# Attention, mixture of experts and feed-forward on one core: another expert order, another order of attention's small products, other queues for the first pairs

## Chip, core and metric

The kernel runs on one core of one Trainium2 chip. The time is the device time of one execution in microseconds (us). Each execution has its own time; the profile comes from one further execution. TensorE is called PE, VectorE DVE, ScalarE ACT, GpSimd POOL, and SyncE SP; a name with a q behind it (SPq, ACTq) is the queue or sequencer of that engine.

## What is computed

Three layers in a row on 2304 tokens of 512 values (4 batches of 576 tokens, 8 heads of 64). Cut to its core:

```python
q_rot, k_rot = rotate(q), rotate(k)                       # rotary positions
attn = softmax(q_rot @ k_rot.T / sqrt(64));  x = attn @ v # per batch and head
x = x.transpose(0, 2, 1, 3).reshape(2304, 512)

xn, en = x / (norm(x) + 1e-6), expert_emb / (norm(expert_emb) + 1e-6)
logits = xn @ en.T / tau;  expert_idx = argmax(logits, 1)  # 8 experts
for e in range(8):                                         # each token goes to one expert
    out[expert_idx == e] = gate * (relu(x @ w1[e]) @ w2[e])  # 512 -> 1024 -> 512

h = out @ w_in;  g = where(h > 0, h, exp(min(h, 0)) - 1);  y = g @ w_out  # 512 -> 2048 -> 512
```

The reference, evaluated on the inputs that are used, sends 6, 709, 173, 0, 3, 691, 722 and 0 tokens to experts 0 to 7. After the first three of the four batches the counts are 6, 706, 173, 0, 3, 118, 722 and 0.

## The kernel before

**Order.** All work is put down as small tasks, `add(time, function, arguments)`, with a due time in abstract units. `emit` sorts them by that time and writes them out, so the numbers set the order of the instructions on every engine and on every queue. An engine takes its instructions in this order. `OFF` is a table of corrections to due times, and of choices such as which engine does a step.

**Attention** runs in 16 pairs of heads, 9 units apart. For pair p: `load` brings q and k (and both with their halves swapped) on SP's queue; `rope` is six steps on POOL or DVE; `hi` (ACT) and `lo` (DVE) split the result into two float16 parts; `stack` copies these with six DMAs into one of four operand buffers. `sc` (line 327) makes score products, and `sc_max` (line 337, DVE) takes the largest of each row; nine of these per pair. `m_turn` (lines 347 and 348, "the turn of the maxima") transposes the maxima on PE, ACT copies them (line 350), and two small DMAs (lines 352 and 353, on ACT's queue) put them beside the operands. Then come nine `st` (lines 363 and 364), the scores again in transposed form with the maximum subtracted, each followed by an exponential on ACT (line 365). `pv` makes, for each of five blocks of keys, the product with v (line 401) and right behind it the sums of the exponentials (line 409). `o_out` copies the result, `o_turn` (line 427, "the turn of the output") transposes it on PE, and `epi` (lines 442 to 451, DVE) divides by the sums. sc, st and both turns take their place in PSUM from a ring of three double banks (`pair`): each use waits until the use three places back in the ring has been read.

**Routing** follows each batch: logits, the place of each token in its expert's list (`r_*`), and a scatter of the tokens. `tab_early` (after three batches) and `tab_head`, `tab_visits`, `tab_compact` (after four) work out on DVE which expert each visit serves. A **visit** is one block of up to 128 tokens of one expert. The first five visits are settled by `tab_early`. `tab_head` ranks the experts by their blocks that are left (`rk`, 0 for the most; the expert that the early visits ended with gets rank 0), and subtracts 3.5 from ranks of 4 and over, so that small experts stand between large ones. With the counts above there are 22 visits, and their experts are 1 six times, 0, 5 six times, 4, 6 six times, 2 twice. There is room for 25; those from the 19th on are skipped on PE by a branch if they aren't used, and small products (line 1083) stand in.

**Expert stage.** Visit j has `mm1` (lines 1057 to 1059, 96 products), `relu` on ACT and DVE, `mm2` (lines 1094 to 1096, 24 products) and `y_out`. On PE, mm2 of a visit follows mm1 of the next one. Where a visit's expert is another than that of the visit before, `w_load` brings its 4 MB in eight pieces (lines 1009 and 1012, SP's queue) into staging buffers, and `w_conv` splits each into float16 parts on ACT (line 1029) and DVE (line 1031). There are eleven staging buffers at first. One after the other they are given up for the third layer's weights (list `until`), at the due time of the first weight chunk that is put there. From unit 36.3 of this stage (two units are one visit) there are two.

**The third layer's weights** come as 64-bit floats in 32 chunks. `widen` turns a chunk into float16 parts, in five steps that go ACT (line 960), DVE (lines 962 to 965), ACT (968), POOL or DVE (971 to 974, chunks 16 and up), ACT (981), POOL (983). `WT` gives each chunk its due time, in units of the stage. Chunks 16 to 29 stand at 23.6, 30, 30.9, and so on up to 42.2. Two chunks can be under way.

**Third layer.** Nine groups of 256 tokens: `ff1` (lines 1139 to 1141), `elu`, `ff2` (1191 to 1193), `fold`, `store`.

## Time and profile before

| | us |
|---|---|
| median of 3 runs | 1009.29 |
| lowest and highest | 1006.53, 1009.57 |
| the profiled execution: its time | 1010.61 |
| the profiled execution: its span, first to last instruction | 1008.8 |
| PE busy in it | 901.2 |
| DVE, ACT, POOL busy | 669.7, 502.3, 546.3 |

The span falls into these stages: the first pairs' way to PE, up to about 44 us; attention until about 356; the change to the experts, which overlaps it, until 372.5; the visits until about 634; and the third layer. All times in rows are us from the span's start. A row of a timeline gives start, duration, engine, line, operation, what is written and read, how many instructions are merged in the row and, in brackets, how long the engine had stood idle before and what ended that. MH are the maxima, ms their transposed copy; most other things lie in one large tile, arena. PEclk in a table of stretches is the granted clock of PE as a share of full speed (1.0 is 2.4 GHz, 0.5 is 1.2 GHz).

### The profile page before, as it was taken

How to read it: one execution, taken by the hardware profiler on the slowest of the kernel's cores; microseconds unless marked ns; L12 is line 12 of the kernel's file. 1: busy time of each engine (PE TensorE's matmuls, PEld its weight loads, DVE VectorE, ACT ScalarE, POOL GpSimd, SP SyncE). 2: the span in 40 equal slices, each digit the busy share in tenths (PEclk: the TensorE clock that was granted, in tenths of full speed). 3: DMA queues.
4: the chain of work that ended last, by engine and by line, in shares of the span. 5: the costliest groups of instructions: out<-in, count | busy, mean ns of one | idle time of the engine just before them, and what ended most of it. 6: DMA issues, size and time to landing. Idle time of an engine off the chain costs nothing. (4 is left out here: it accounts for less than half of the span.)

```text
span 1008.8 us, 24500 instructions
## 1 busy us (share of the span) xinstructions
PE 901.2 (89%) x9398; PEld 655.4 (65%) x9398; DVE 669.7 (66%) x1070; ACT 502.3 (50%) x858; POOL 546.3 (54%) x652
## 2 busy tenths in 40 slices
PE   3398999998989779999999876998999999999994
PEld 0154555554445467776776652887888888888884
DVE  8556757867868547778786874775665565664651
ACT  1244464464464633565665444645555555555540
POOL 6475565685643203424428544366776765766640
PEclk8588999999999979999999987999999999999998
DMA  7554465584463844997997674401201202201000
GB/s 261 152 166 107 129 156 136 142 200 127 133 144 104 251 85 144 328 249 200 260 304 175 192 203 92 123 2 43 64 22 43 64 22 43 65 22 44 22 22 21
DMA packets 127094, 127.65 MB, mean 127 GB/s; under 512 B 71272, under 2 KB 105064, under 8 KB 126960
## 3 DMA queue, kind: packets, MB, share of 16 engines
q1 hardware_dynamic: 118000, 97.68, 37.5%
q0 software_dynamic: 8352, 27.62, 8.5%
q8 instruction: 76, 1.25, 0.5%
q10 hardware_dynamic: 608, 0.63, 0.2%
q14 instruction: 58, 0.48, 0.2%
HBM read 79.15 MB, written 17.35 MB: 96 GB/s over the span
## 5 line engine op out<-in xcount | busy, mean ns | idle before, releaser
L1139 PE MATMUL banks<-arena 128*128 128x256 f16 x576 | 157.1, 273 | 2.4 <-ACT arena L1154 2.4
L1141 PE MATMUL banks<-arena 128*128 128x256 f16 x576 | 157.1, 273 | 0.0
L1140 PE MATMUL banks<-arena 128*128 128x256 f16 x576 | 157.1, 273 | 0.0
L365 ACT ACTIVATE arena<-banks 128x576 f32<-128x576 f32 x144 | 89.8, 652 | 125.8 <-PE banks L364 108.5
L1191 PE MATMUL banks<-arena 128*128 128x256 f16 x504 | 138.2, 274 | 5.5 <-DVE arena L1206 5.5
L1174 DVE TENSOR_TENSOR arena<-arena 128x896 f16<-128x896 f32 x72 | 79.9, 1110 | 89.0 <-ACT arena L1170 84.0
L1192 PE MATMUL banks<-arena 128*128 128x256 f16 x504 | 138.2, 274 | 0.0
L1193 PE MATMUL banks<-arena 128*128 128x256 f16 x504 | 138.2, 274 | 0.0
L1170 ACT ACTIVATE arena<-arena 128x896 f16<-128x896 f32 x71 | 67.5, 951 | 122.7 <-POOL arena L1167 121.4
L337 DVE TENSOR_REDUCE MH<-banks 128x1 f16<-128x576 f32 x144 | 103.2, 751 | 34.1 <-PE banks L327 32.3
L1059 PE MATMUL banks<-arena 128*128 128x128 f16 x704 | 122.4, 222 | 1.5 <-DVE arena L1031 1.5
L1057 PE MATMUL banks<-arena 128*128 128x128 f16 x704 | 122.5, 222 | 0.0
L1058 PE MATMUL banks<-arena 128*128 128x128 f16 x704 | 122.5, 222 | 0.0
L1164 POOL TENSOR_TENSOR arena<-arena 128x256 f32<-128x256 f32 x67 | 54.1, 808 | 91.4 <-DVE arena L1161 91.4
L983 POOL TENSOR_TENSOR arena<-arena 128x896 f16<-128x896 f32 (+1 forms) x32 | 51.6, 1611 | 86.1 <-ACT arena L981 65.7
L401 PE MATMUL banks<-arena 128*64 128x256 f32 (+9 forms) x768 | 90.9, 362 | 4.6 <-DVE arena L377 4.6
L363 PE MATMUL banks<-arena 128*128 128x288 f16 (+1 forms) x320 | 79.5, 299 | 3.5 <-DVE l L523 2.2
L327 PE MATMUL banks<-arena 64*128 64x288 f16 (+1 forms) x320 | 48.5, 313 | 37.0 <-DVE MH L337 16.2
L1095 PE MATMUL banks<-arena 128*128 128x512 f16 x176 | 70.2, 399 | 10.2 <-DVEq L993 9.6
L364 PE MATMUL banks<-arena 128*128 128x288 f16 (+1 forms) x320 | 78.5, 294 | 0.0
L1094 PE MATMUL banks<-arena 128*128 128x512 f16 x176 | 69.8, 396 | 6.0 <-ACT arena L1069 4.4
L377 POOL TENSOR_TENSOR arena<-arena 128x576 f16<-128x576 f32 x26 | 30.2, 1162 | 79.8 <-ACT arena L365 79.8
(238 smaller groups left out, 2285.2 us busy)
## 6 DMA issues: line engine op xcount, KB each, us to landing
arena<-in_w_dram SPq DMA_DIRECT2D x48, 512.0 KB
arena<-in_qk_dram SPq DMA_DIRECT2D x30, 576.0 KB
arena<-in_wo_dram SPq DMA_DIRECT2D x32, 256.0 KB
arena<-in_wi_dram SPq DMA_DIRECT2D x16, 512.0 KB
arena<-arena SPq DMA_DIRECT2D x32, 216.0 KB
yreg<-arena POOLq DMA_DIRECT2D x25, 260.0 KB, 4.0
arena<-arena SPq DMA_DIRECT2D x32, 144.0 KB
arena<-in_vp_dram SPq DMA_DIRECT2D x16, 256.0 KB
```

The costliest lines, as they stand in the source:

```text
L337: nc.vector.tensor_reduce(out=MH1[p % 2][:, c:c + 1], in_=t[:, :, 0:288], op=ALU.max, axis=AX.XY, negate=True)
L365: nc.scalar.activation(P32[:, (9 * p + i) % RP].rearrange("p (c n) -> p c n", c=2), t[:, :, 0:288], AF.Exp, scale=2.0)
L401: nc.tensor.matmul(o[64 * e:64 * e + 64, c, 0:QC[c].stop - QC[c].start], lhsT=w, rhs=x[:, QC[c]], start=first and n == 0, stop=end and n = ...
L1057: nc.tensor.matmul(o[:, fc], lhsT=w[:, 0, a], rhs=x[:, k], start=k == 0, stop=False)
L1058: nc.tensor.matmul(o[:, fc], lhsT=w[:, 0, a], rhs=x[:, 4 + k], start=False, stop=False)
L1059: nc.tensor.matmul(o[:, fc], lhsT=w[:, 1, a], rhs=x[:, k], start=False, stop=k == 3)
L1139: nc.tensor.matmul(o[:, v], lhsT=wih[k][:, f0:f0 + 128], rhs=z[:, :, k], start=k == 0, stop=False)
L1140: nc.tensor.matmul(o[:, v], lhsT=wih[k][:, f0:f0 + 128], rhs=z[:, :, 4 + k], start=False, stop=False)
L1141: nc.tensor.matmul(o[:, v], lhsT=wil[k][:, f0:f0 + 128], rhs=z[:, :, k], start=False, stop=k == 3)
L1191: nc.tensor.matmul(y, lhsT=a, rhs=b, start=u + f + n == 0, stop=False)
L1192: nc.tensor.matmul(y, lhsT=a, rhs=w[:, 1, WB[i - 1]], start=False, stop=False)
L1193: nc.tensor.matmul(y, lhsT=q[:, 1, f, GB[i - 1]], rhs=b, start=False, stop=u + f == 4 and n == len(m) - 1)
```

## The change

**Expert order.** `tab_head` gets two more steps on DVE: the expert of rank 2 has 7 added to its rank and so is visited last. With the counts above the visits become 1 six times, 0, 5 six times, 4, 2 twice, 6 six times. Chunks of the third layer get other due times: 26 and 27 at 23.2 and 29, then 16 to 25, 28 and 29 from 34 to 43.35, 0.85 apart. The staging buffers whose place they take are so kept longer: seven are there until 33.9, and three or more until 40.7.

**Attention.** The sums become a task `ps` of their own, due up to 0.8 later than the product with v, so that one st mostly stands between them. The turn of the maxima moves from 2.9 to 3.68 units after the last maximum, and the turn of the output from 14.7 to 15.05, so that both stand right in front of the next sc. From the second pair on, the two DMAs of the maxima are issued by SP and not by ACT.

**First pairs.** The order of what all queues do for pairs 0 to 3 is another: c_prep's conversion of constants goes to ACT, the rest of c_prep and the norm of the expert embeddings move behind; all six rope steps of pair 0, and three of pair 2, are DVE's; pair 1 has a buffer of its own for its float16 parts; pair 0's stack is eight DMAs, four on SP and four on ACT; three warm-up products fewer. The score products of pair 1 stand behind the first st of pair 0 and not before it.

```diff
+    def c_copy():
+        nc.scalar.copy(c16, cft[:, 0:512])
     def c_prep():
-        nc.vector.tensor_copy(c16, cft[:, 0:512])
...
         if w == 0:
-            hlt[p] = at("hl", F16, 4, 576)
+            hlt[p] = at("P", F16, 4, 576, add=32256) if p == 1 else at("hl", F16, 4, 576)
...
     def stack(p):
+        if p == 0:
+            for e, eng in ((0, nc.sync), (1, nc.scalar)):
+                a, o = slice(64 * e, 64 * e + 64), slice(64 - 64 * e, 128 - 64 * e)
+                eng.dma_start(out=t[a, e, 0:3:2, 0:576], in_=h[a, 0:3:2])
...
-        nc.scalar.dma_start(out=d[64:65, 0, 1], in_=ms[0:5])
-        nc.scalar.dma_start(out=d[0:1, 1, 1], in_=ms[5:10])
+        eng = nc.sync if p else nc.scalar
+        eng.dma_start(out=d[64:65, 0, 1], in_=ms[0:5])
+        eng.dma_start(out=d[0:1, 1, 1], in_=ms[5:10])
...
+        po[p, kt] = ones
+    def ps(p, kt):
+        o, ones, end = obank, po.pop((p, kt)), kt == PVO[-1]
         for c in range(2):
...
+        pl_ = tbv(864, 8)
+        nc.vector.tensor_scalar(pl_, rk, 2.0, 7.0, op0=ALU.is_equal, op1=ALU.mult)
         nc.vector.tensor_tensor(rk, rk, ps_, op=ALU.add)
+        nc.vector.tensor_tensor(rk, rk, pl_, op=ALU.add)
...
-    add(-25.5, warm, OFF.get('WN', 13))
+    add(-25.5, warm, 10)
...
-        u, w = (z - 13.45, 1) if p else (z - 19, .3)
+        u, w = {0: (-19, .3), 1: (.6, .6), 2: (6.2, .95)}.get(p, (z - 13.45, 1))
...
-        add(u + w * (UT[4] + (2.9 if p else 1.3)), m_turn, p)
+        add(u + w * (UT[4] + (3.68 if p else 1.3)), m_turn, p)
...
+            add(z + t + (.01 if p == NP - 1 else ST5[kt]), ps, p, kt)
-        add(z + (11.8 if p < NP - 1 else 10.6), o_out, p)
-        e = z + (14.7 if p < NP - 1 else 11.4)
+        add(z + (12.3 if p < NP - 1 else 10.6), o_out, p)
+        e = z + (15.05 if p < NP - 1 else 11.4)
...
-    WT |= dict(zip(range(16, 30), (23.6, 30, 30.9, 31.8, 32.7, 33.6, 34.5, 35.4, 36.3, 37.2, 38, 39.3, 40.2, 42.2)))
+    WT |= dict(zip((26, 27, 16, 17, 18, 19, 20, 21, 22, 23, 24, 25, 28, 29), (23.2, 29, 34, 34.85, 35.7, 36.55, 37.4, 38.25, 39.1, 39.95, 40.8, 41.65, 42.5, 43.35)))
...
-        n = min((0, 1, 2, 3) if c < 20 else (0, 1, 2) if c < 28 else (2, 4), key=lambda n: last[n])
+        n = min((0, 1, 2, 3) if t < 35 else (0, 1, 2) if c < 28 else (2, 4), key=lambda n: last[n])
```

In the changed file the lines are numbered anew: line 178 is c_prep's conversion in both, 280 to 284 are rope (277 to 281 before), 293 is lo (290), 338 sc (327), 348 sc_max (337), 352 and 358, 359 the step before the turn of the maxima and that turn (341, 347, 348), 375 and 376 st (363, 364), 415 the product with v (401), 427 the sums (409), 445 the turn of the output (427).

DVE at the start, before, from the second lo of pair 0 to the first four maxima of pair 0 (281 is pair 1's rope, 227 to 235 the embeddings' norm):

```order
L178 CAST c_67<-cft 128x512
L179 MEMSET tot 128x8
L180 RECIPROCAL rtau<-taut 128x1
L181 MEMSET chg 128x25
L182 TENSOR_SCALAR rtau<-rtau 128x1
L281 TENSOR_TENSOR arena<-arena 128x576
L227 TENSOR_SCALAR n_100<-n_100 8x1
L229 RECIPROCAL n_100<-n_100 8x1
L231 TENSOR_SCALAR arena<-arena,n_100 8x512
L233 CAST arena<-arena 8x512
L235 TENSOR_TENSOR arena<-arena 8x512
L337 TENSOR_REDUCE MH_92<-banks 128x1 x4
```

The same place in the changed kernel, from the last steps of pair 0's rope to pair 1's second lo (280 and 284 behind the two lo are pair 1's):

```order
L284 TENSOR_TENSOR arena<-arena 128x576
L293 TENSOR_TENSOR arena<-arena 128x576 x2
L280 TENSOR_TENSOR arena<-arena 128x576
L284 TENSOR_TENSOR arena<-arena 128x576
L348 TENSOR_REDUCE MH_92<-banks 128x1 x4
L293 TENSOR_TENSOR arena<-arena 128x576
L348 TENSOR_REDUCE MH_92<-banks 128x1 x5
L352 COPY MH_94<-MH_92 128x1
L293 TENSOR_TENSOR arena<-arena 128x576
```

Eleven steps that stood between pair 0's last lo and its first maximum are gone from there; two rope steps of pair 1 stand there now, and pair 1's second lo follows the ninth maximum directly.

PE at the start, before, from the turn of pair 0's maxima on (twelve products of line 327, three sc of pair 1, stand before the first st of pair 0):

```order
L347 MATMUL banks<-c_67,MH_92 10x128
...
L348 MATMUL banks<-c_67,MH_94 10x128
...
L327 MATMUL banks<-arena 128x288
...
L363 MATMUL banks<-arena 128x288
...
L364 MATMUL banks<-arena 128x288
```

The same place in the changed kernel (four products of lines 375 and 376, then four of line 338, and so on in turns):

```order
L358 MATMUL banks<-c_67,MH_92 10x128
...
L359 MATMUL banks<-c_67,MH_94 10x128
...
L375 MATMUL banks<-arena 128x288
...
L376 MATMUL banks<-arena 128x288
...
L338 MATMUL banks<-arena 128x288
```

The first st of pair 0 now follows the turn directly, and no product of pair 1 stands in front of it.

PE in the middle of attention, before, around the two turns (363 and 364 are st, 327 sc, 401 the product with v, 409 the sums):

```order
L409 MATMUL banks<-arena,one_86 32x192 x4
...
L363 MATMUL banks<-arena 128x288
...
L347 MATMUL banks<-c_67,MH_93 10x128
...
L348 MATMUL banks<-c_67,MH_95 10x128
L427 MATMUL banks<-cft,arena 128x128 x8
...
L364 MATMUL banks<-arena 128x288
...
L327 MATMUL banks<-arena 128x288
```

The same place in the changed kernel:

```order
L376 MATMUL banks<-arena 128x288
L427 MATMUL banks<-arena,one_86 32x128 x4
L427 MATMUL banks<-arena,one_86 32x192 x4
...
L375 MATMUL banks<-arena 128x288
...
L358 MATMUL banks<-c_67,MH_93 10x128
...
L359 MATMUL banks<-c_67,MH_95 10x128
L445 MATMUL banks<-cft,arena 128x128 x8
...
L338 MATMUL banks<-arena 128x288
...
L415 MATMUL banks<-arena 64x256 x2
```

Both turns now stand one st later, and the sc that stood behind turn and st follows the turn of the output directly; one st stands between the product with v and its sums.

## Rows read from the trace of the kernel before

**Rows 1.** Stretches: length, busy PE, PEld, DVE, ACT, POOL (count), PEclk, DMA, GB/s.
```profile
50.00:345.00 295.00, 270.94 (x3294) 151.26 (x3293) 206.27 (x368) 152.18 (x292) 173.07 (x142) 0.96 0.57 152
372.50:570.00 197.50, 197.50 (x2261) 146.45 (x2257) 150.69 (x240) 110.08 (x159) 86.61 (x115) 0.99 0.82 223
570.00:634.00 64.00, 46.42 (x331) 25.01 (x329) 42.50 (x64) 29.83 (x42) 28.38 (x39) 0.84 0.58 162
```

**Rows 2.** Waits of PE: who for whom, us in total, times, longest.
```profile
PE banks L327 <- DVE arena L451: 7.0, 10, 0.7
PE banks L427 <- DVE MH L337: 6.5, 6, 2.0
```

**Rows 3.** Timeline of PE, first pairs.
```profile
16.74 0.66 PE L327 MATMUL banks<-arena 64*128 64x288 f16 x4 [0.65 <-DMA arena<-arena]
23.24 1.06 PE L327 MATMUL banks<-arena 64*128 64x288 f16 x4 [5.84 <-DVE MH L337]
29.25 0.27 PE L347 MATMUL banks<-c,MH 128*10 128x128 f16 x1 [1.30 <-DVE MH L337]
37.00 0.42 PE L327 MATMUL banks<-arena 64*128 64x288 f16 x1 [7.29 <-DMA arena<-arena]
44.09 0.40 PE L363 MATMUL banks<-arena 128*128 128x288 f16 x1
```

**Rows 4.** Timelines of DVE, ACT's queue and SP's queue, first pairs.
```profile
12.69 4.90 DVE L178 CAST c<-cft 128x512 f16<-128x512 f32 x1
22.45 2.73 DVE L337 TENSOR_REDUCE MH<-banks 128x1 f16<-128x576 f32 x4
33.85 0.76 DVE L290 TENSOR_TENSOR arena<-arena 128x576 f16<-128x576 f32 x1 [4.46 <-ACT arena L286]
31.35 0.70 ACTq L353 DMA_DIRECT2D arena<-ms  x1
33.84 1.25 SPq L296 DMA_DIRECT2D arena<-arena  x2
```

**Rows 5.** Timeline of PE in mid-attention: turns of the output, st, waiting sc.
```profile
189.77 1.09 PE L427 MATMUL banks<-cft,arena 128*128 128x128 f32 x8 [0.29 <-DVE MH L337]
190.70 0.29 PE L363 MATMUL banks<-arena 128*128 128x288 f16 x1
...
191.29 0.29 PE L327 MATMUL banks<-arena 64*128 64x288 f16 x1
192.29 0.40 PE L327 MATMUL banks<-arena 64*128 64x288 f16 x3 [0.71 <-DVE arena L451]
```

**Rows 6.** Timeline of PE: mm1 of two visits, 17 apart; first ff1.
```profile
385.73 0.22 PE L1057 MATMUL banks<-arena 128*128 128x128 f16 x1
...
564.91 0.22 PE L1057 MATMUL banks<-arena 128*128 128x128 f16 x1
...
630.81 0.28 PE L1139 MATMUL banks<-arena 128*128 128x256 f16 x1
```

**Rows 7.** Last expert's weights: SP's queue, ACT's conversion.
```profile
572.47 5.83 SPq L1009 DMA_DIRECT2D arena<-in_w_dram  x4
602.09 1.06 ACT L1029 ACTIVATE arena<-arena 128x1024 f16<-128x1024 f32 x1 [3.21 <-DMA arena<-in_w_dram]
```

**Rows 8.** Widening on DVE (chunks 17, 25) and POOL; PE's wait behind it.
```profile
526.45 0.43 DVE L962 TENSOR_SCALAR arena<-arena 128x512 f32<-128x512 f32 x1
571.12 0.43 DVE L962 TENSOR_SCALAR arena<-arena 128x512 f32<-128x512 f32 x1
567.47 0.44 DVE L963 TENSOR_SCALAR arena<-arena 128x512 uint32<-128x512 uint32 x1
571.59 2.08 DVE L963 TENSOR_SCALAR arena<-arena 128x512 uint32<-128x512 uint32 x1
571.50 1.88 POOL L983 TENSOR_TENSOR arena<-arena 128x896 f16<-128x896 f32 x1 [2.50 <-ACTq L993]
577.13 0.38 PE L1095 MATMUL banks<-arena 128*128 128x512 f16 x1 [2.65 <-DVEq L993]
```

More of the change, by code (lines that the diff above doesn't have):

```diff
@@ L229, in emb_norm @@
             nc.vector.reciprocal(n8[:, 1:2], n8[:, 1:2])
+            nc.vector.tensor_scalar(n8[:, 1:2], n8[:, 1:2], 32.0, None, op0=ALU.mult)
         elif i == 4:
-            nc.vector.tensor_scalar(et, et, n8[:, 1:2], 32.0, op0=ALU.mult, op1=ALU.mult)
+            nc.scalar.activation(et, et, AF.Copy, scale=n8[:, 1:2])
         elif i == 5:
-            nc.vector.tensor_copy(eh[:, 0], et)
+            nc.scalar.copy(eh[:, 0], et)
         else:
@@ L377, in p_lo @@
         eng.tensor_tensor(lo_slot(p, i), P32[:, r], PHB[:, r], op=ALU.subtract)
+    po = {}
     def pv(p, kt):
@@ L797 @@
     for i in range(7):
-        add((-24.2, -24, -21.2, -21.1, -21, -20.9, -20.8)[i], emb_norm, i)
-    add(4, emb_turn)
-    add(-25.5, warm, OFF.get('WN', 13))
+        add((3.5, 5.5, 9.2, 9.3, 10.4, 11.4, 12.4)[i], emb_norm, i)
+    add(17.4, emb_turn)
+    add(-25.5, warm, 10)
     for s, t in enumerate((-37, -36.9, -36.8, -36.7)):
         add(t, d_prep, s)
-    add(-22.0, c_prep)
+    add(-24.55, c_copy)
+    add(-10.1, c_prep)
     VT = (4.6, 6.2, 7.7, 9.6, 11.4)
     UT = [t - VT[0] for t in VT]
+    ST5 = (.7, .02, .5, .7, .8)
     for p in range(NP):
@@ L810 @@
         add(z - 39, load, p, 0)
-        add(z - 36 if p else z - 38.5, load, p, 1)
+        add({0: z - 38.5, 4: 1}.get(p, z - 36), load, p, 1)
         for i in range(6):
-            add(g - 33.3 + 1.5 * i if p else g - (33, 32.9, 32.85, 33, 32.8, 32.5)[i], rope, p, i)
-        for f, i, t in ((hi, 0, -26.1), (lo, 0, -25), (hi, 1, -20.6), (lo, 1, -19.4)) if p else ((hi, 0, -25.6), (lo, 0, -24.6), (hi, 1, -24.5), (lo, 1, -23.6)):
-            add(g + t, f, p, i)
-        add(g - (19.3 if p else 23.5), stack, p)
-        u, w = (z - 13.45, 1) if p else (z - 19, .3)
+            add((-23.3, -22.8, -21.3, -20.5, -19.3, -18.1)[i] if p == 1 else g - 33.3 + 1.5 * i if p else g - (33, 32.9, 32.85, 32.84, 32.8, 32.5)[i], rope, p, i)
+        ht = {0: (-25.6, -24.6, -24.5, -23.6, -23.5), 1: (-18.2, -18, -16.8, -16.5, -16.4), 2: (-8.2, -7, .4, .8, .9), 3: (4.8, 5.2, 6.4, 7.6, 7.7)}
+        ht = ht.get(p, tuple(g + t for t in (-26.04, -25, -20.54, -19.4, -19.3)))
+        for f, i, t in zip((hi, lo, hi, lo), (0, 0, 1, 1), ht):
+            tasks.append((t, len(tasks), f, (p, i)))
+        tasks.append((ht[4], len(tasks), stack, (p,)))
+        u, w = {0: (-19, .3), 1: (.6, .6), 2: (6.2, .95)}.get(p, (z - 13.45, 1))
         u += OFF.get(f'u@{p}', 0)
@@ L839 @@
             for g in range(5):
-                add(z - 34 + 3 * g + 6 * (b == 0), v_load, b, g)
+                add(-18.9 if b == 0 and g == 4 else z - 34 + 3 * g + 6 * (b == 0), v_load, b, g)
                 add(z - 25 + 3 * g + 6 * (b == 0), v_hi, b, g)
@@ L857 @@
             for t in range(5):
-                add(y + 2 + t, r_sq, b, 0, 0, 384, t)
+                add(y + 1.5 + .9 * t, r_sq, b, 0, 0, 384, t)
         if p % 4 == 3:
@@ L887 @@
                 zt = q + dt * len(ops) + .1
-                steps(zt, .12, 21, tab_head)
+                steps(zt, .11, 23, tab_head)
                 steps(zt + 2.7, .1, 10, tab_visits)
```

10 lines of the change are left out of this document (8 added, 2 removed).

## The prediction

> **What bounds the kernel now.** I read the stretches first, then PE's waits, then the timelines where PE stands still. Where all runs well, PE sets the pace: in the first 197.5 us of the visits it is busy for 197.50 [rows 1]. So what can be won is PE's idle time, and it lies in three places. At the start the first st comes only at 44.09 [rows 3]. In attention PE is busy for 270.94 of 295.00 us [rows 1]; the waits list names 7.0 us in which sc waits for `epi` (line 451) and 6.5 in which the turn of the output waits for maxima (line 337) [rows 2]. At the end of the visits PE is busy for 46.42 of 64.00 us, at a mean granted clock of 0.84 [rows 1]. The third layer, from the first ff1 at 630.81 [rows 6] to the end at 1008.8, is 378.0 us; none of its code changes, and it only moves.
>
> **Expert order.** Visits run at (564.91 - 385.73) / 17 = 10.54 us each; that row is mm1 of the 20th visit [rows 6]. Two more visits and one mm2 (half a visit) behind it would end at 564.91 + 2 x 10.54 + 10.54 + 5.3 = 601.8, since on PE mm2 of the 21st and mm1 of the 22nd make a visit's length too. With 1 us for the products that stand in for unused visits, ff1 could start at 603. It starts at 630.81: 27.8 us are lost. The reason is in the last weights' timelines [rows 7]. The expert of the 21st visit is a new one, only two staging buffers are left by then, its first pieces are asked for at 572.47, and ACT still waits for its second half at 602.09. With the new order that expert (2) is visited 15th and 16th, and the last change, to expert 6, is at the 17th visit, when seven buffers stand ready; behind it no weights are loaded. Before, changes at the 14th and 15th visit lay in the stretch in which PE was never idle [rows 1], with six buffers. I cost the third change in a row at nothing: the seven buffers hide it, and without them it would cost what the last change costs now. The two steps more in `tab_head` lie beside dense visits on PE: nothing.
>
> What the widening takes back. Chunks 17 to 25 went through DVE from 526.45 to 571.12, eight steps of 5.58 us [rows 8]; planned were 0.9 units, 4.74. The 16th visit's mm1 is at 385.73 + 13 x 10.54 = 522.8 (unit 30), so chunk 17's DVE step, due 0.52 units later at 525.5, came 0.9 late, and chunk 25's, due at 563.5, came 7.6 late. That is when PE starts to wait for DVE's queue, 2.65 us at 577.13 [rows 8]: relu stands in that queue behind the widening. So about 8 us of lateness are free, and what is beyond that PE waits for. Now 12 chunks stand 0.85 units (4.48 us) apart: 11 steps at 5.58 are 61.4 us, planned 49.3, lateness at the last one 0.9 + 12.1 = 13. Beyond the free 8 that is 5 us. With 1 us for the third change this part gives 27.8 - 6, **22 us**. Its bounds: 28 if the widening keeps its plan, and 5 by the first rival.
>
> Here a rule speaks against the change. At 571.59 DVE's step of line 963 took 2.08 us, beside POOL's subtraction of 1.88 us that had begun at 571.50; at 567.47 the same step took 0.44 [rows 8]. The Trainium skill ("SBUF — State Buffer", section "Who interferes with whom") says that a tensor_scalar in a two-port mode and a GpSimd instruction take one shared pair of ports for a whole instruction, and that the second to issue fully blocks. By that rule chunks packed closer meet more often, and the sum would go toward the first rival; by the mean pace of the eight steps, collisions included, it stays at 22.
>
> **Attention's order.** sc waits ten times for `epi`, 7.0 us [rows 2], because its second bank is the one that the turn of the output used three places back, with one st between: the turn at 189.77, st from 190.70, one product at 191.29, the others held until 192.29 [rows 5]. Now the ring gives sc the banks of an st and of the turn of the maxima, and the output's bank goes to the st that follows sc, product and sums. These take longer than the 0.71 that was missing, so all 7.0 go. The turn of the output waited six times, 6.5 us in all and 2.0 at most, for the maxima of the next pair's first sc [rows 2]. Now the turn of the maxima takes that bank, and it stands one st later, 191.29 - 190.70 = 0.59 us [rows 5]. Six times 0.59 are at most 3.5; a short wait such as the 0.29 [rows 5] has less to lose: 2.7. Given back: sc now needs ACT's copy of the maxima directly behind the turn of the output. That turn is 1.09 long and covers most of it; per pair the cost is between nothing and the old 0.7, and I take 0.15, for 15 pairs 2.2. The two DMAs of the maxima, now on SP's queue behind loads and ahead of the next stack, stop ACT for 0.70 less each [rows 4]; the st that needs them stands about five small products behind the turn, which I take to cover the way over SP: nothing. The sums set apart change no duration: nothing. Together **7.5 us**, bounds 0 and 10.
>
> **First pairs.** Pair 0's first product is whole at 16.74 + 0.66 = 17.4 [rows 3], yet DVE takes the first maxima at 22.45, because c_prep's conversion alone holds it for 4.90 us from 12.69 [rows 4], and other steps follow; PE's next sc waits for it 5.84 [rows 3]. In the new order nothing of that stands ahead. The stack can go some 0.7 us sooner, since rope is DVE's alone and its second part needs fewer bytes, so the first product is whole at about 16 and the maxima start soon after. From there to the turn it is 29.25 - 22.45 = 6.8 us as before, so the turn is at about 23.1. The DMAs of the maxima end their issue at 32.05 [rows 4], 2.8 us behind the turn. Their landing isn't seen; pair 1's stack, issued from 33.84 [rows 4], lets PE go at 37.00 [rows 3], 3.2 later, and these are far smaller: 2.5, between 1 and 3.2. That puts the first st at 23.1 + 2.8 + 2.5 = 28.4, and not at 44.09, **15.7 us sooner**, since the three sc of pair 1 don't stand before it any more; they waited 7.29 us [rows 3] for a stack whose last `lo` came at 33.85 [rows 4], behind all maxima of pair 0. Given back are these three sc: six maxima of 2.73 / 4 = 0.68 us [rows 4] and the products, 2 us each, since the two hardly overlap with a ring of three: 5.7. Net **10 us**, bounds 3 (pair 2 not ready, second rival) and 16 (all three hidden between st). The conversion on ACT waits for the constants' load ahead of pair 0's second `hi`: between nothing and 1 us, inside these bounds. Three warm-up products fewer lie before 16.74, where PE waits for DMA: nothing. The embeddings' norm is needed only by the first batch's logits: nothing.
>
> **Sum.** 22 + 7.5 + 10 = 39.5. The profiled execution took 1010.6, so 971.1. The median of the three runs is 1.3 below it: **970 us**. The first ff1 should come at 591.
>
> **Rivals.**
> *The widening sets the pace of the last visits.* If each step loses what 571.59 shows, 2.08 - 0.44 = 1.6 us, to POOL, the pace is 7.2; 11 steps are 79, lateness 31, 23 beyond the free 8, and the expert part gives 5: 987. For it: that row. Against: the eight steps already hold such meetings. By the skill's rule above this is the way it goes. 0.15.
> *The second and third pair aren't ready.* Their rope (POOL), loads and stacks may set the pace instead of PE; then the start gives 2 or 3 and the time is 977. For it: pair 1's stack was late already [rows 3]. Against: half of pair 2's rope is moved to DVE. 0.14.
> *More than that.* The widening keeps up, the sc of pair 1 hide: 28 + 9 + 15 = 52: 957. 0.18.
> *Slower: SP's queue.* The DMAs of the maxima stand in SP's queue behind a load that waits until a q and k buffer is free. If rope falls behind, that load holds them, the st of every pair waits, and the pairs behind it get later still. It outweighs the gains from 39.5 / 15 = 2.6 us a pair; at 4 it gives 1009.3 + 60 - 39.5 = 1030. For it: nothing else on SP's queue stood between ACT's copy and st before. Against: the load's buffer is free some four units ahead. 0.04.
> *The order isn't what it says,* since counts set it at run time, or the 17th visit's weights are late and cost what the 21st's did: gain of the expert part halved: 981. 0.05.
>
> **How the numbers follow.** The forecast has 0.44, with 962 to 976 as its own range. Below 952 lie the upper bounds all at once, above 990 the slow case and the far end of the first rival, together under 0.2: range 952 to 990. A measurement here tells 0.3% (3 us) from no change; only the slow case is slower, and no change would need the gains cancelled to within 3 us: faster 0.94, same 0.02, slower 0.04.
>
> **What would show it.** First st near 28 and turn of pair 0's maxima near 23; no sc waiting for `epi`, and under 4.5 us of waits of both turns; the last load of expert weights before 540, and no wait of ACT's conversion of over 3 us; first ff1 near 591 and 378 us from there to the end. It is wrong if the first ff1 comes after 605, if PE waits for the DMAs of the maxima in most pairs, or if PE idles over 10 us in the last five visits.

## The result, and the profile after

| | before | after |
|---|---|---|
| median (4 runs each) | 1007.92 | 998.39 |
| lowest and highest | 1006.53, 1009.57 | 994.09, 1000.93 |
| the profiled execution: its time, its span | 1010.61, 1008.8 | 1000.93, 999.0 |

The ratio is 0.9894, with a 95% interval of 0.987 to 0.9918. Two later batches of runs gave 0.9884 (0.9846 to 0.9922) and 0.9900 (0.9865 to 0.9934). The change is faster by some 10 us; 39 were forecast, and 998 lies above the range of 952 to 990. The first ff1 comes at 615.87; after 605 was a sign of being wrong that the prediction had named.

Four stretches tell where the 10 us are. The rows give length, busy PE, PEld, DVE, ACT, POOL, the clock, DMA share and GB/s. First before: from the turn of pair 1's output to that of pair 12's, on to mm1 of the third visit, on to the first ff1, and on to the end.

```profile
93.40:305.10 211.70, 192.46 (x2319) 106.85 (x2319) 154.19 (x250) 108.46 (x211) 126.29 (x100) 0.97 0.58 144
305.10:385.73 80.63, 67.87 (x902) 46.58 (x903) 49.83 (x150) 38.42 (x78) 22.74 (x27) 0.89 0.50 147
385.73:630.81 245.08, 227.50 (x2434) 158.58 (x2432) 181.72 (x259) 135.63 (x192) 108.89 (x144) 0.96 0.80 216
630.81:1008.80 377.99, 356.66 (x3242) 317.03 (x3241) 221.83 (x316) 188.22 (x320) 230.26 (x329) 0.98 0.16 41
```

The same stretches of the changed kernel:

```profile
91.80:289.80 198.00, 186.44 (x2320) 103.66 (x2318) 148.54 (x250) 111.87 (x213) 128.73 (x101) 0.99 0.59 152
289.80:377.30 87.50, 69.20 (x900) 46.80 (x899) 51.77 (x151) 37.84 (x76) 23.16 (x27) 0.88 0.47 140
377.30:615.87 238.57, 222.16 (x2433) 157.73 (x2432) 184.02 (x254) 131.42 (x188) 111.80 (x140) 0.97 0.80 221
615.87:999.00 383.13, 358.68 (x3242) 318.37 (x3241) 224.20 (x321) 190.94 (x324) 232.59 (x334) 0.98 0.16 42
```

Up to pair 1's turn the change gave 1.6 us (10 forecast for the first pairs). Middle attention gave 13.7 (7.5 forecast): 7.7 of idle time and 6.0 of busy time. The mean granted clock rose from 0.97 to 0.99 there, which by these shares is some 4 of the 6.0 (0.03 of 211.7 us against 0.01 of 198.0); the rest isn't explained. Its end lost 6.9. The visits gave 6.5 (22 forecast), and the third layer lost 5.1.

Five rows of the list of PE's waits (who for whom, total, times, longest), to set beside [rows 2]:

```profile
PE banks L376 <- DMA arena<-ms: 11.3, 2, 6.2
...
PE banks L375 <- DVE MH L348: 9.9, 6, 7.0
PE banks L1123 <- ACTq L1022: 9.0, 2, 7.6
...
PE banks L1168 <- ACT arena L1183: 4.5, 2, 3.5
PE banks L1124 <- DVEq L1022: 4.3, 2, 3.2
```

Both waits of [rows 2] are gone from the list: sc for `epi`, and the turn of the output for maxima. Of these five, those of mm2 (1123 and 1124, 13.3 us) were there before too, with 15.5 us (lines 1094 and 1095):

```profile
PE banks L1095 <- DVEq L993: 9.6, 3, 4.0
PE banks L1094 <- ACT arena L1069: 4.4, 1, 4.4
PE banks L1094 <- ACTq L993: 1.5, 2, 1.1
```

The places of the five on PE in the changed kernel (start, duration, in brackets the wait ahead; lines 375 and 376 are st, 1086 mm1, 1123 and 1124 mm2, 1168 ff1):

```profile
28.18 0.42 PE L376 MATMUL banks<-arena 128*128 128x288 f16 x1 [5.16 <-DMA arena<-ms]
55.48 0.40 PE L375 MATMUL banks<-arena 128*128 128x288 f16 x1 [6.99 <-DVE MH L348]
324.50 0.40 PE L376 MATMUL banks<-arena 128*128 128x288 f16 x1 [6.15 <-DMA arena<-ms]
377.30 0.22 PE L1086 MATMUL banks<-arena 128*128 128x128 f16 x1
601.78 0.58 PE L1123 MATMUL banks<-arena 128*128 128x512 f16 x1 [7.64 <-ACTq L1022]
605.55 0.59 PE L1124 MATMUL banks<-arena 128*128 128x512 f16 x1 [3.19 <-DVEq L1022]
615.87 0.28 PE L1168 MATMUL banks<-arena 128*128 128x256 f16 x1
640.65 0.27 PE L1168 MATMUL banks<-arena 128*128 128x256 f16 x1 [3.52 <-ACT arena L1183]
```

The row at 28.18 is the first st that needs the maxima, as forecast (28.4). The others, mm1 and the first ff1 aside, are places where the gain went. At 55.48 PE waits for pair 2's maxima; DVE (first row) and POOL show why:

```profile
45.60 9.16 DVE L293 TENSOR_TENSOR arena<-arena 128x576 f16<-128x576 f32 x1
45.11 1.39 POOL L280 TENSOR_TENSOR arena<-arena 128x576 f32<-128x576 f32 x1
46.48 1.14 POOL L389 TENSOR_TENSOR arena<-arena 128x576 f16<-128x576 f32 x1
47.58 1.39 POOL L282 TENSOR_TENSOR arena<-arena 128x576 f32<-128x576 f32 x1
48.94 1.14 POOL L389 TENSOR_TENSOR arena<-arena 128x576 f16<-128x576 f32 x1
50.04 1.39 POOL L284 TENSOR_TENSOR arena<-arena 128x576 f32<-128x576 f32 x1
51.40 1.39 POOL L280 TENSOR_TENSOR arena<-arena 128x576 f32<-128x576 f32 x1
52.75 1.39 POOL L282 TENSOR_TENSOR arena<-arena 128x576 f32<-128x576 f32 x1
54.22 1.79 POOL L284 TENSOR_TENSOR arena<-arena 128x576 f32<-128x576 f32 x1
```

DVE's step (pair 3's second lo) takes 0.75 us elsewhere. Here it ends at 54.76, 0.62 us after POOL's row has its first gap, 52.75 + 1.39 = 54.14 to 54.22. At 324.50 PE waits for the last pair's maxima; ACT's copy, then SP's queue:

```profile
312.78 0.24 ACT L361 CAST ms<-banks 10x128 f16<-10x128 f32 x1
313.96 2.32 SPq L1038 DMA_DIRECT2D arena<-in_w_dram  x4
316.38 0.80 SPq L364 DMA_DIRECT2D arena<-ms  x1
317.23 0.67 SPq L365 DMA_DIRECT2D arena<-ms  x1
```

SP issues four loads of the first expert's weights ahead of the DMAs of the maxima, though these have been ready since 313.0. The issue of both DMAs ends at 317.9, and st goes 6.6 us later. The widening: the first and the last of its twelve late chunks on DVE, then ACT's step that waits for POOL, and relu behind it:

```profile
539.42 0.43 DVE L991 TENSOR_SCALAR arena<-arena 128x512 f32<-128x512 f32 x1
607.82 0.42 DVE L991 TENSOR_SCALAR arena<-arena 128x512 f32<-128x512 f32 x1
600.25 0.95 ACT L1010 ACTIVATE arena<-arena 128x896 f16<-128x896 f32 x1 [1.62 <-POOL arena L1003]
601.11 0.58 ACT L1098 ACTIVATE arena<-banks 128x512 f16<-128x512 f32 x1
```

(607.82 - 539.42) / 11 = 6.22 us a chunk, planned 4.48. PE's mm2 of the last visit, at 601.78, waits for this relu, whose products were there at 586.9.

### The profile page after: what moved, and what is told of

The parts are those of the page before. It is cut to its first block, busy times and chain, and to the rows that moved or that the text cites. A ratio compares the mean times of both kernels' runs of the same rounds, so it can differ in the third digit from the quotient of the medians.

```text
span 999.0 us, 24589 instructions
## 1 busy us (share of the span) xinstructions
PE 893.6 (89%) x9395; PEld 652.7 (65%) x9395; DVE 677.7 (68%) x1073; ACT 506.4 (51%) x861; POOL 549.6 (55%) x649
## 3 DMA queue, kind: packets, MB, share of 16 engines
q10 hardware_dynamic: 756, 1.04, 0.3%
## 5 line engine op out<-in xcount | busy, mean ns | idle before, releaser
L377 ACT ACTIVATE arena<-banks 128x576 f32<-128x576 f32 x144 | 93.3, 652 | 106.1 <-PE banks L376 100.2
L375 PE MATMUL banks<-arena 128*128 128x288 f16 (+1 forms) x320 | 81.4, 300 | 12.7 <-DVE MH L348 9.9
L376 PE MATMUL banks<-arena 128*128 128x288 f16 (+1 forms) x320 | 80.4, 297 | 11.3 <-DMA arena<-ms 11.3
L1123 PE MATMUL banks<-arena 128*128 128x512 f16 x176 | 68.0, 386 | 9.0 <-ACTq L1022 9.0
L1086 PEld LDWEIGHTS <-arena 128*128 128x128 f16 x704 | 70.2, 100 | 2.7 <-issue 0.3
L1088 PEld LDWEIGHTS <-arena 128*128 128x128 f16 x704 | 70.2, 100 | 2.5 <-DVEq L1022 1.9
L1124 PE MATMUL banks<-arena 128*128 128x512 f16 x176 | 68.0, 386 | 4.3 <-DVEq L1022 4.3
```

What stands on the lines that cost most here:

```text
L377: nc.scalar.activation(P32[:, (9 * p + i) % RP].rearrange("p (c n) -> p c n", c=2), t[:, :, 0:288], AF.Exp, scale=2.0)
L1086: nc.tensor.matmul(o[:, fc], lhsT=w[:, 0, a], rhs=x[:, k], start=k == 0, stop=False)
L1088: nc.tensor.matmul(o[:, fc], lhsT=w[:, 1, a], rhs=x[:, k], start=False, stop=k == 3)
```

## Experiments

All marks are from one trace per kernel, in us: mm1 of the third visit; from it to the first ff1; from there to the end; and the last two together. Ratios are to the kernel before, run in the same batch. Batches ran on different chips (the kernel before had 1008 to 1017), so ratios are compared within a batch (first letter). One trace is no exact measure: three of the changed kernel (first batch, f0, k0) have 621.7, 621.6 and 618.4 in the column "both". In e1, e2, e3, g1 and g2 this column also holds a wait of PE of 4.08, 1.59, 3.66, 2.50 and 2.44 us for a transposed load near 400 us, which in the others is 0.7 at most.

| kernel | third visit | to ff1 | to end | both | ratio |
|---|---|---|---|---|---|
| before | 385.7 | 245.1 | 378.0 | 623.1 | |
| changed | 377.3 | 238.6 | 383.1 | 621.7 | 0.9894 |
| e1_ms15 | 362.7 | 246.1 | 382.6 | 628.6 | 0.9813 (0.9754 to 0.9872) |
| e2_lo3 | 368.7 | 239.2 | 384.3 | 623.6 | 0.9837 (0.9786 to 0.9888) |
| e3_nowiden | 366.5 | 224.9 | 376.4 | 601.3 | 0.9556 (0.9506 to 0.9605) |
| e4_pace | 366.9 | 225.9 | 397.8 | 623.7 | 0.9838 (0.9788 to 0.9888) |
| f0_after | 374.5 | 238.1 | 383.4 | 621.6 | 0.9884 (0.9846 to 0.9922) |
| f1_wdt3 | 369.1 | 238.5 | 383.2 | 621.7 | 0.9944 (0.9917 to 0.9972) |
| f2_no_order | 374.9 | 244.3 | 379.6 | 623.8 | 0.9894 (0.9845 to 0.9943) |
| f3_order_only | 385.6 | 240.6 | 384.7 | 625.3 | 1.0007 (0.9985 to 1.0028) |
| g1_adds | 373.0 | 241.2 | 383.1 | 624.3 | 0.9832 (0.9793 to 0.9871) |
| g2_half | 371.5 | 231.4 | 379.5 | 611.0 | 0.9645 (0.9586 to 0.9705) |
| g3_attn | 372.8 | 247.4 | 377.5 | 624.9 | 0.9839 (0.9815 to 0.9863) |
| k0_after | 370.8 | 237.5 | 380.9 | 618.4 | 0.9900 (0.9865 to 0.9934) |
| k1_two_repairs | 365.4 | 238.4 | 383.4 | 621.8 | 0.9806 (0.9781 to 0.9830) |
| k2_late_four | 364.2 | 224.6 | 396.9 | 621.5 | 0.9810 (0.9777 to 0.9842) |
| k3_attn_act | 366.9 | 245.6 | 379.1 | 624.7 | 0.9852 (0.9824 to 0.9879) |
| m1_no_dve | 363.7 | 237.2 | 383.3 | 620.4 | 0.9743 (0.9651 to 0.9834) |
| m2_no_adds | 366.0 | 230.6 | 380.4 | 611.0 | 0.9680 (0.9602 to 0.9758) |

### The parts of the change

**f2_no_order and f3_order_only.** The expert part (rank step, `WT`, choice of load buffer) taken out of the changed kernel, and put alone into the kernel before:

```diff
-        nc.vector.tensor_tensor(rk, rk, pl_, op=ALU.add)
-    WT |= dict(zip((26, 27, 16, ...), (23.2, 29, 34, 34.85, ...)))
+    WT |= dict(zip(range(16, 30), (23.6, 30, 30.9, ...)))
```

> The changed kernel with the expert order, the chunks' due times and so the staging buffers as they were before: attention's order and the first pairs alone are changed. By the two first profiles the expert part was worth 6.5 us up to the first ff1 (238.6 and not 245.1 from the third visit's mm1) and lost 5.1 in the third layer (383.1 and not 378.0). Theory A (the widening ate the gain): first ff1 245 behind the third visit, third layer 378, and the time is 0 to 4 us above the changed kernel's. Theory B (the prediction's sum, 22 us, holds beside other losses): 15 us and more above it.

> The kernel before with the new expert order, the chunks' new due times and the staging buffers that follow from them, and nothing else of the change. Theory A (the widening ate the gain): the third visit's mm1 stays at 384 to 387, first ff1 comes 236 to 241 behind it, the third layer takes 381 to 385, and the time is 0 to 4 us below the kernel before. Theory B (the 22 us are there when attention is as before): first ff1 223 to 227 behind the third visit, and the time 18 us and more below.

Theory A both times: the expert part is worth nothing, 1.0007 alone. In f3 the first ff1 comes 4.5 us earlier behind the third visit, and the third layer takes 6.7 longer. PE's longest wait at the end of f3's visits, beside the 2.65 of [rows 8]:

```profile
612.14 0.59 PE L1099 MATMUL banks<-arena 128*128 128x512 f16 x1 [7.60 <-ACTq L998]
```

**g3_attn.** Attention's new order alone, on the kernel before (`ps`, both turns, DMAs of the maxima on SP; the squares for pair 14's norm move as in the change):

```diff
-        add(u + w * (UT[4] + (2.9 if p else 1.3)), m_turn, p)
+        add(u + w * (UT[4] + (3.68 if p else 1.3)), m_turn, p)
```

> The kernel before with attention's new order alone (the sums apart, both turns in front of the score products, the DMAs of the maxima on SP from the second pair on). Theory A (the predicted 7.5 us are there, but the last pair's DMAs behind the weight loads take some 6 back): from the turn of pair 1's output to that of pair 12's 198 to 202 us and not 211.7, a wait of 4 to 8 us for the DMAs in the last pair, the third visit's mm1 at 379 to 384 and not 385.7, time 2 to 6 us below the kernel before. Theory B (no loss at the end): third visit at 373 to 377, time 8 us and more below. Theory C (the order wins only together with the earlier first pairs): 208 us and more between the two turns, time within 2 us.

Theory B, nearly: the third visit is at 372.8, the two turns are 199.1 us apart (89.3 to 288.4), and the last DMAs cost a wait of 2.67 only (2.60 and 3.56 in g1 and g2, the same batch; 6.2 to 8.2 in the first batch, f and k). Its ratio, 0.9839, is that of g1, a kernel with the whole change, in the same batch. Attention's order carries the gain; which of its parts does isn't told apart, and the new first pairs were not run alone. Pair 1's turn, at 89.3, is 4.1 us earlier than before with the old first pairs.

### The first pairs and the last pair

**f0_after and k0_after.** The changed kernel again.

> The changed kernel once more, beside the three that follow. In its first profile one DVE step of the first pairs lasted 9.16 us (the second lo of pair 3, from 45.60); in three kernels with the same first pairs it lasted 3.10 to 3.43 us. Theory A (how long DVE is held there hangs on whether POOL's row of steps happens to have a gap, so it differs from run to run): 2.5 to 4 us or about 9 us, and with the short one the third visit's mm1 is at 365 to 368 and not at 377. Theory B (the first profile is the rule, and the other kernels shifted it): about 9 us and 377 again.

> The changed kernel a third time, beside the three that follow. In five traces of kernels with its first pairs one DVE step there (the second lo of pair 3) lasted 5.9 to 10.1 us, in three 3.1 to 3.4. Expected again: anywhere between; with over 9 us the turn of pair 1's output at 88 to 92 and the third visit's mm1 at 373 to 378, with under 4 us at 83 to 84 and 365 to 368.

DVE's step took 9.09 us in f0 and 1.11 in k0, so it differs between executions of one program. With the short one the third visit came at 370.8, later than the 365 to 368 expected; k0 has a wait of 7.79 us for the last pair's DMAs. In e1, which has the same first pairs, it took 3.15, and POOL's row has its gap sooner:

```profile
45.76 3.15 DVE L293 TENSOR_TENSOR arena<-arena 128x576 f16<-128x576 f32 x1
46.89 1.40 POOL L282 TENSOR_TENSOR arena<-arena 128x576 f32<-128x576 f32 x1
48.77 1.15 POOL L389 TENSOR_TENSOR arena<-arena 128x576 f16<-128x576 f32 x1 [0.48 <-ACT arena L377]
```

The gap, 0.48 us from 48.29, is there because ACT's exponential came late for POOL. So the step's length hangs on when POOL happens to wait. With a step of 1.1 to 3.4 us (k0, e1, e3, e4) the turn of pair 1's output is at 83.2 to 84.1; with 9 and more (f0, g1, the first profile) at 88.6 to 91.8. In f1 and g2 it was pair 3's first lo that was held, for 5.9 and 6.0 us, and the turn is at 86.3 and 87.2. The step isn't all: in f2, with 1.04 us, the turn is at 88.7, and that stays open.

**e1_ms15.**

```diff
-        eng = nc.sync if p else nc.scalar
+        eng = nc.sync if 0 < p < NP - 1 else nc.scalar
```

> The changed kernel, but the two DMAs of the last pair's maxima are issued by ACT again. In the changed kernel the last pair's first st waits 6.15 us for them (from 318.35 to 324.50), and the third visit's mm1 comes at 377.30. Theory A (SP's queue: the DMAs stand behind four weight loads of the first expert, which SP issues from 313.96): the wait is under 1.5 us, PE's clock doesn't fall behind it, the third visit's mm1 comes at 368 to 371, and the time falls by 6 to 9 us. Theory B (the weights that are under way hold the DMA engines, whichever queue issues): the wait stays over 4 us and the time moves by less than 2 us. Theory C (DVE's routing chain sets when the visits start): the wait goes, but the third visit comes after 375.

The wait is gone and the third visit is at 362.7, 3.8 us ahead of e3, which has the same front: theory A, with half its size. In the eleven traces with these DMAs on SP the last pair waits 2.5 to 8.2 us for them, in the eight with them on ACT not at all. The time of e1 shows little of it: it is 4 us below e2 and e4, which have them on SP (994.6 against 998.3 and 998.4), within their spread, and in its trace PE waits 4.08 us for a transposed load at 398.98.

**e2_lo3.**

```diff
-        nc.vector.tensor_tensor(h[:, 2 * w + 1], qkt[p][:, 2 * w], h[:, 2 * w], op=ALU.subtract)
+        eng = nc.gpsimd if (p, w) == (3, 1) else nc.vector
+        eng.tensor_tensor(h[:, 2 * w + 1], qkt[p][:, 2 * w], h[:, 2 * w], op=ALU.subtract)
```

> The changed kernel, but one step, the second lo of pair 3, is done by POOL and not by DVE. In the changed kernel it lasts 9.16 us on DVE, from 45.60, while POOL goes through rope steps without a gap; the maxima of pair 2 stand behind it on DVE, and PE waits 6.99 us for them at 55.48. Theory A (POOL's row of steps holds that one DVE instruction off): no DVE step of over 4 us is left there, the 6.99 us wait is under 1.5, the turn of pair 1's output comes at 83 to 86 and not at 91.8, and the time falls by 6 to 9 us. Theory B (the second and third pair aren't ready, and this step is only where it shows): waits of 5 us and more turn up behind it, the turn of pair 1's output comes after 89, and the time falls by less than 3 us.

Inconclusive alone: in this batch the other traces had a short step too, so there was nothing to repair; the turn of pair 1's output is at 86.5, later than theirs (83.2 to 83.7).

**k1_two_repairs.** Both edits together.

> The changed kernel with two edits together: the last pair's DMAs of the maxima back on ACT's queue, and the second lo of pair 3 done by POOL. Theory A (both cost what their traces showed, some 4 us for the DMAs and 5 to 8 for DVE's long step where it occurs): no DVE step of over 4 us in the first pairs, no wait for the DMAs of the maxima after 100 us, the third visit's mm1 at 361 to 365, the time 5 to 12 us below the changed kernel in this call. Theory B (what is won ahead of the visits is lost in them, since the widening ends when it ends): the same third visit, but the time within 3 us.

Theory A by its time: 989.28 (988.17 to 990.49) against 997.19 (991.18 to 1002.24) for the changed kernel in the same batch. It beats both kernels. The hold itself isn't repaired: in k2 and m1 below, which have both edits, another subtraction on DVE (line 390, the low part of the exponentials) is held beside POOL's row for 7.37 and 6.57 us, and PE waits 6.21 and 5.42 us for DVE behind it. In k2 (line 416 is the product with v, and L229 the small step that follows the held one):

```profile
48.36 7.37 DVE L390 TENSOR_TENSOR arena<-arena 128x576 f16<-128x576 f32 x1
55.77 1.39 PE L416 MATMUL banks<-arena 128*64 128x256 f16 x9 [6.21 <-DVE n L229]
```

The turn of pair 1's output is at 86.4 in k1 and at 87.0 to 88.6 in k2, m1 and m2, no earlier than in many traces without the edit. Which of the two edits does how much was not timed apart.

**k3_attn_act.** g3 with e1's line.

> The kernel before with attention's new order alone, and the last pair's DMAs of the maxima on ACT's queue. Attention's order alone gave a third visit at 372.79, with a wait of 2.67 us for these DMAs and a time 16 us (1.6%) below the kernel before. Theory A: no such wait, third visit at 367 to 371, time 17 to 22 us below the kernel before. Theory B (the wait's place is taken by another): third visit 371 to 374, time 14 to 17 below. If this comes out as fast as the changed kernel or faster, the new first pairs and the expert order are worth nothing in the mean.

Third visit at 366.9 and no such wait (A); the time is 14.3 us below the kernel before (B's edge). It is as fast as the changed kernel or faster. k1, which adds the new first pairs and the expert order to it, is 4.9 us faster (989.28 against 994.22); in the two traces 1.5 of that lie ahead of the third visit and 2.9 behind it, which is no more than traces of one kernel differ by.

### Why the expert order gained nothing

**e3_nowiden and g2_half.** The last twelve chunks, or every second of them, not widened (the edit of e3; in g2 the condition is `t >= 34 and c % 2`; `blank` fills a chunk's place with constants):

```diff
         for i in range(5):
-            addv(t + WO[i] * d, widen, c // 16, c % 16, i)
+            if t < 34:
+                addv(t + WO[i] * d, widen, c // 16, c % 16, i)
+        if t >= 34:
+            addv(t, blank, c % 16)
```

> The changed kernel with the widening of the last twelve chunks left out (16 to 25, 28 and 29: their loads stay, their places are filled with constants by POOL, so the output is another). Theory A (the widening sets the pace of the last visits): PE stays dense to the end of the visits, the first ff1 comes at 594 to 598 and not at 615.87, the third layer takes 378 us again and not 383, and the time is 973 to 978. Theory B (the skipped visits, the branches on DVE and ACT, or the expert order itself hold PE): the first ff1 comes after 608 and the time is over 988.

> The changed kernel with the widening of six of the last twelve chunks left out (17, 19, 21, 23, 25 and 29; their places are filled with constants by POOL, so the output is another), the rest at the same due times, so 1.7 units (9 us) apart. With all twelve left out the stretch from the third visit's mm1 to the end was 601.3 us, with all twelve in it 621.5. Theory A (a chunk takes 6.2 us of pace, and PE is only held where they are planned closer than that): nothing is held now, the stretch is 600 to 603. Theory B (the widening's work itself is paid for, chunk by chunk): half of the 20 us comes back, the stretch is 609 to 613.

e3: theory A. Without the widening, and apart from the 3.66 us for a transposed load at 401.90, PE is dense to the end of the visits; first ff1 is at 591.33, and both stretches fall from 621.7 to 601.3. So these twelve chunks cost 20 us (24 with that wait taken off), about the 22 that I had promised to the expert order. g2: half of the price, as B says, though ACT waits in it six times for a chunk's load, 1.5 to 5.1 us each.

**e4_pace, k2_late_four, f1_wdt3, g1_adds.** Wider spacing; the last four chunks behind the first ff1; a third buffer; the additions on DVE:

```diff
-(23.2, 29, 34, 34.85, 35.7, 36.55, 37.4, 38.25, 39.1, 39.95, 40.8, 41.65, 42.5, 43.35)
+(23.2, 29, 34, 35.15, 36.3, 37.45, 38.6, 39.75, 40.9, 42.05, 43.2, 44.35, 45.5, 46.65)   # e4
+(23.2, 29, 34, 35.1, 36.2, 37.3, 38.4, 39.5, 40.6, 41.7, 50.6, 51.8, 53, 54.2)   # k2
-    wdt = Turns([at("PL", U32, 7, 128, add=8192 + 3584 * i) for i in range(2)])
+    wdt = Turns([at("PL", U32, 7, 128, add=8192 + 3584 * i) for i in range(3)])   # f1
-'WQ': (0, 1, 2, 3, 4, 8, 12, 14, 15)
+'WQ': (14, 15)   # g1
```

> The changed kernel with the last twelve chunks 1.15 units (6.06 us) apart and not 0.85 (4.48), from the same start, so that the last one is due at 46.65 and not at 43.35. In the changed kernel they go through at 6.22 us each. Theory A (a due time that the widening can't keep puts its waiting steps ahead of relu and y_out in the queues of ACT and DVE; at the pace it can keep PE isn't held): the first ff1 comes at 597 to 604 and the time falls by 10 to 18 us. Theory B (the work of the widening itself is too much beside the visits, whatever its order): the first ff1 stays within 4 us of 615.87, the time within 4 us. Theory C (the second half of the weights then comes too late): the first ff1 comes early, but the first ff2 waits 5 us and more, and the third layer takes over 388.

> The two repairs, and the last twelve chunks in another place: 16 to 23 from 34 on, 1.1 units apart, and 24, 25, 28 and 29 at 50.6 to 54.2, behind the first ff1 (due at 50). Theory A (the 20 us are lost because the last chunks fall due where no product is left to cover them, in the skipped visits): first ff1 224 to 228 behind the third visit's mm1, the third layer 380 to 388, the stretch from the third visit to the end 606 to 614 and not 621 to 624. Theory B (moved chunks cost as much beside the first elu, which ACT, DVE and POOL must do as well): first ff1 as early, but the third layer 394 or more, the stretch 619 to 626.

> The changed kernel with three buffers for the last steps of a widened chunk and not two, so that a third chunk can enter DVE's third step (line 993) before POOL has ended the first one's subtraction (line 1012). Theory A (two chunks under way, each 12.5 us from its first step to its last, set the pace of 6.2 us): the last twelve chunks go through DVE at 5.2 us or less each, first ff1 comes 228 to 232 us behind the third visit's mm1 and not 238.6, and the time falls by 5 to 10 us. Theory B (the order in the queues sets it: each step stands behind others that wait): the pace stays over 5.9 us and the time within 3 us.

> The changed kernel with the four additions of every late chunk on DVE (lines 1000 to 1003), where chunks 16 to 20, 24 and 28 had them on POOL: about 1.15 us on DVE in place of 2.6 on POOL, so that each of these chunks is through sooner and meets fewer POOL instructions. The late chunks went through at 6.06 to 6.27 us each in six traces, also with a third buffer. Theory A (the length of one chunk's way through the engines sets the pace): pace 5.7 or less, first ff1 229 to 234 behind the third visit's mm1 and not 238, time down by 4 to 8 us. Theory B (DVE's queue sets the pace, where relu and the conversion stand too): pace 6.0 to 6.6, first ff1 237 to 243 behind, time within 3 us.

None changes the sum of both stretches, 621.5 to 624.3. e4 and k2 make the visits dense (225.9 and 224.6) and pay it all back in the third layer, 397.8 and 396.9, where ff1 waits for elu behind the widening; one wait each, e4 then k2:

```profile
618.73 0.37 PE L1168 MATMUL banks<-arena 128*128 128x256 f16 x1 [5.80 <-ACT arena L1183]
661.22 0.37 PE L1169 MATMUL banks<-arena 128*128 128x256 f16 x1 [6.01 <-ACT arena L1184]
```

In e4 the chunks, planned 6.06 us apart, went through 6.87 apart. A third buffer doesn't change the pace (6.27), nor do additions on DVE (6.13). f1 is slower by its ratio, which its trace, of the fastest of its ten runs, doesn't explain; that stays open.

**m1_no_dve and m2_no_adds.** On k1, from the twelve chunks DVE's four steps taken out, or the four additions:

```diff
+        elif i == 1 and w == 1 and c in LATE:   # m1
+            nc.scalar.activation(df[:, 0:512], a.bitcast(F32), AF.Copy)
...
-            if w == 1:   # m2
+            if w == 1 and c not in LATE:
```

> The kernel with the two repairs, in which the four DVE steps of the twelve late chunks (lines 991 to 994, some 2.3 us a chunk) are left out and one copy on ACT of some 0.65 us stands in, so the output is another; all other steps and the order of the queues stay. The stretch from the third visit's mm1 to the end was 618 to 625 us in all kernels with the whole widening, 611 with half of the chunks, 601 with none. Theory A (DVE's share of the work is what costs): 603 to 610. Theory B (the chain of steps over three engines, in the order of the queues, is what costs, and a step gone shortens it by little): 614 to 621.

> The kernel with the two repairs, in which the four additions of the twelve late chunks (lines 1000 to 1003: 2.6 us on POOL in seven chunks, 1.2 on DVE in five) are left out, so the output is another. Theory A (DVE's share is what costs; here DVE loses 6 us in all): 616 to 621 from the third visit to the end. Theory B (the length of the chain costs; here each chunk's is 1.2 to 2.6 us shorter): 606 to 614.

DVE's steps can go, with a copy of some 0.65 us on ACT in their place, and nothing changes (620.4; 621.8 in k1); the additions give 10.8 us (611.0), half of the price. So it isn't the work of DVE's four steps, nor their meetings with POOL; theory B, on the additions' side. That nothing is gained when DVE does the additions (g1), though that is shorter, suggests that their place between two ACT steps counts as well as their length; the two aren't told apart.

## Why the prediction was wrong, step by step

**Expert order, 22: measured 0.** The step that failed is what the widening takes back: I had put it at 5 us, and e3 shows 20 (621.7 against 601.3). I had seen that weights and widening were both late in [rows 7, 8] and gave nearly all of the 27.8 us to the weights. Three parts of the term were wrong. The pace of 5.58 us was read from chunks that were planned 4.74 apart; the new plan of 4.48 ran at 6.22, so the last chunk lost 19 us on its plan and not 12. The 8 us of free lateness did not hold: by them the 7 us more would still leave 15 of the 22, and up to the first ff1 there were 6.5. And what lateness costs isn't over at the first ff1: elu stands behind the same steps, 5.1 us that I had counted as a third layer that only moves. What was right: the last weights are no longer late (the last load is issued at 527, forecast before 540), and the first rival names the place. Its mechanism, DVE's meetings with POOL, fell with m1: the meetings are there (the four steps took 3.1 us a chunk, 2.2 at their shortest), but without these steps the stretch is the same. With it fell the sentence that, by the Trainium skill's rule, it goes that way because of them.

**Attention, 7.5: 13.7 between the turns.** Both waits are gone, and idle time fell by 7.7. That this meets the 7.5 is partly luck: between the turns the two waits of [rows 2] are 6.3 and 6.5 us, and both went whole, where I had counted 2.7 of the second; and 4.7 came back in other waits, where I had counted 2.2 for another cause (the largest new one is the turn of the maxima for maxima, 2.9). The other 6.0, of busy time, I had left out; some 4 of it are the clock, granted at 0.99 and not 0.97.

**The last pair, nothing: 4 to 7.** "Nothing" for the DMAs on SP's queue was wrong at one place, and the slow rival had looked at the wrong load: not the one of q and k, but the expert's weights, four of them ahead in the last pair. The stretch with the 6.15 us wait took back half of what attention won; its mean clock, 0.88, was 0.89 before.

**First pairs, 10: 6.1 at best, a loss at worst.** Turn at 22.21 (forecast 23.1) and st at 28.18 (28.4) came as worked out. But attention's order alone already puts the turn of pair 1's output at 89.3 and 89.2 (g3, k3), so the new first pairs gave 5.2 to 6.1 us there with a short DVE step (turn at 83.2 to 84.1) and lost 2.5 in the first profile (91.8). The term that failed is the 5.7 us given back for pair 1's sc. From st to the turn PE took 57.5 us in k0, with a short step, and 45.2 in g3, where the first pairs are as before: 12.3 given back, and in the first profile, with 63.7, more still. The two st, k0 first:

```profile
26.59 0.42 PE L376 MATMUL banks<-arena 128*128 128x288 f16 x1 [3.41 <-DMA arena<-arena]
44.18 0.40 PE L364 MATMUL banks<-arena 128*128 128x288 f16 x1
```

What takes the time with a short step isn't told apart. With a long one it is also POOL's fuller row, which I had taken as free. The Trainium skill ("SBUF — State Buffer", section "Who interferes with whom") says that a DVE instruction with two SBUF inputs contends with a GpSimd instruction that reads SBUF. The trace agrees, with 9.16 us for a subtraction of 0.75, and shows more: DVE was held over the POOL instruction that ran when it started and six more, not one. [rows 4] had shown DVE held beside POOL already: c_prep's conversion, which on ACT takes 0.62 us, took 4.90 on DVE and ended at 17.59, just behind the first gap of POOL's row (17.30):

```profile
15.91 1.39 POOL L279 TENSOR_TENSOR arena<-arena 128x576 f32<-128x576 f32 x1
17.38 1.46 POOL L281 TENSOR_TENSOR arena<-arena 128x576 f32<-128x576 f32 x1
```

**The range.** It left out that two rivals could come true together (the widening and the second pair), which gives 994; I had added their chances, not their prices. That 994 is near 998 is partly luck: the loss in the last pair and the third layer's 5.1 stood in no rival, and attention gave 6.2 us more than forecast.

## What to carry to other kernels

When a stall has two late things behind it, the gain of curing one is bounded by the other: leave the other out on the chip, or at least read its pace where it runs freely, before the whole stall goes into the sum. Here work that several engines pass on in fixed queues cost the same wherever it was moved, spaced or buffered, and only leaving out chunks or the additions gained; compare the stretch that holds all its places, not the one where the wait was seen. Before DMAs change queue, list what that queue issues at every place where they stand, the last one above all.

## What the runs showed of the hardware

A DVE subtraction of two SBUF tensors was held off for the whole of an unbroken row of POOL instructions: 9.16, 9.09 and 10.12 us in three traces, and less in others, where a gap came sooner. (One got through in 1.72 us, from 41.60, while POOL ran an instruction of 8x1.) In eleven traces the held subtraction (pair 3's second or first lo, or line 390) ended 0.61 to 0.63 us after the end of POOL's row. Maxima read from PSUM ran at their usual length beside the same row (1.42 us for two at 44.26, against 1.43 at 57.23). That the hold differs between executions of one program, 9.16, 9.09 and 1.11 us in three traces of the changed kernel, with pair 1's turn at 91.8, 88.6 and 84.1, I had not expected. And in the last pair PE waited 2.5 to 8.2 us for two DMAs of 1.2 KB in the eleven traces in which SP issues them behind four of 512 KB, and not at all in the eight in which ACT issues them.
